# One order of weight loads two tiles ahead, the last block's sums over three groups, output weights reloaded in pairs, 28 tiles joined early

## The chip, the cores and the metric

The kernel runs on one core of one Trainium2 chip. The metric is the device time of one execution in microseconds (us), as the median of several executions. Engines: PE is TensorE (matmuls), PEld its weight loads, DVE is VectorE, ACT is ScalarE, POOL is GpSimd, and SP is the queue that issues nearly all DMAs. Each engine runs its instructions in the order of the program.

## What is computed

The reference has three parts, one after the other. Inputs q, k and v are float32, all weights are float64.

```python
# retention, 4 batches, 8 heads, 576 positions, 64 per head
scores = (1 / sqrt(64)) * q @ k.T
ret = scores * Dmat            # gamma[h] ** (i - j) for i >= j, else 0
x = (ret @ v)                  # 2304 tokens x 512
# first expert block: w1, w2, w3 are 512 x 768, w_out is 768 x 512
h = max(max(x @ w1, x @ w2), x @ w3)
x = h @ w_out
# second expert block: w_gate, w_val are 512 x 1536, w_out is 1536 x 512
g = x @ w_gate
out = (g * sigmoid(g) * (x @ w_val)) @ w_out
```

## The kernel before, in words

**Precision.** Every large product is made of three float32r matmuls: an operand is split into a high part (ACT copy to float32r) and a low part (DVE or POOL subtract), and high times low, low times high and high times high are added in PSUM. A float64 weight tile (128 partitions x 512, 512 KB) is first joined to float32 from its two words: `f32_steps` (L110) has two ACT operations (L114, L117) and three of DVE (L119, L120, L122). `conv_steps` (L125) adds the split.

**Order.** The program order of all engines is written by hand (`tc.manual_schedule`). Generators carry side work, and `next(...)` at fixed places advances them by one step.

**Stage 1, attention, 32 visits** (`visit`, L371). One visit does the attention of one unit (pair of heads, half a sequence) and, from visit 8, some slices of the first expert block (`f_slice`, L337: 12 matmuls, then ACT L351 or DVE L353 reads the PSUM tile, of which there are two). From visit 16 on each visit has five slices and also advances `early` (L406) two steps before the first slice and one before each later one and at the end, seven in all. `early` joins 22 tiles of the second expert block (tile rows 1 to 11 of w_gate and w_val) and stores the float32 result to `l_d` in DRAM (L417); a tile takes four steps, and its result lies in `wl`, of which there are two (L116). Loads run two tiles ahead; the float64 tile `w64` has three buffers (L103). At even visits `t_load` (L173) puts eight small DMAs on SP.

**Stage 2, remaining slices** (L507): what is left of the slices, while `wo_steps` (L473) loads, joins and splits the six tiles of the first w_out. Its first load is asked for here.

**Stage 3, first output product** (L659 to L691): six half blocks `hx` of 384 tokens, each with four sums `e` of 18 matmuls (L673). After each sum ACT reads it (L678), then `h_split` (L497: ACT high part, POOL low part) makes the operands of the next half block ((0, 1), (2,), (3, 4), (5,) for e = 0 to 3), then four steps of `xsteps` (sums and splits of the block's operands for the next stage) and two of `w_steps([0])`, the preparation of weight tile row 0 of the second expert block: loads (`w_load`, L546), three joins, four sums (L587 to L594) and five splits (L567), each stored to `w_d`.

**Stage 4, second expert block** (`group`, L729). One group takes a tile row `fi` and a block `b` of 768 tokens: seven products of six matmuls (L743) into three PSUM tiles g1 to g3, in the Strassen-like form with operands a, b, c, d, and the gate on ACT, DVE and POOL; then up to three `o()` calls, each an output sum `out2` of six matmuls (L703) of an older pair of tile rows, taken from the list `pend`. Between them ten `hook()` calls advance side work. The order is `seq` (L804): blocks 0 and 1 for all twelve tile rows, and then block 2 alone for tile rows 10, 11, 8, 9, 6, 7, 4, 5, 2, 3, 0, 1, whose weights come back from `w_d` by `w_reload` (L539): a, c, d, b into one buffer for even and one for odd rows, and p (output weights) into four (`wp0` to `wp3`).

In the first group `hook` runs two steps of `x_second(2)`, the last block's sums and splits, whose results go through `xt` (two buffers) and DMA to `x_d` (L626); two of its five splits have their low part on POOL, three on DVE. In the second group `w_steps([1])` runs, again two steps a hook. After that each tile row prepares the next one.

In the last block each group is followed by

```python
        if fi >= GRP:
            w_reload(fi - GRP, "acdbp")
```

Of the kernel before, what the change touches and what calls it, by code (L numbers as in the profile page):

```python
# [22 lines left out]
P = 128  # L23
# [10 lines left out]
GRP = 2  # L34
# [33 lines left out]
def retention_moe(ctx, tc, consts, q, k, v, w1, w2, w3, w_out, w_gate, w_val, w_out2, out):  # L68
# [302 lines left out]
    def visit(n, slices, convs):  # L371
        low = a_value(n)
        if n % 2:
            a_load(n // 2 + 3)
        else:
            t_load(n // 2 + 2)
        if n % (2 * NP) == 2 * NP - 1:
            fq.extend((n // NP - 1 + h, *w) for w in win_units for h in range(2))
        a_state(n + 1)
        low()  # L380
        a_score(n + 1)
        plan = list(conv_plan(convs))
        done = 0
        for j in range(slices + 1):
            if j == min(2, slices - 1) or not slices:
                a_prep(n + 2)
            upto = len(plan) * (j + 1) // (slices + 1)
            for step in plan[done:upto]:
                for i, ph in step:
                    win_phase(i, ph)  # L390
            done = upto
            if n >= 16:
                for _ in range(2 if j == 0 else 1):
                    next(early, None)
            if j < slices:
                f_some(1)

    EARLY = [(fi, wi) for fi in range(1, F2) for wi in range(2)]
# [6 lines left out]

    def early_steps():  # L406

        ld = {}
        last = None
        for i, x in enumerate(EARLY):  # L410
            for y in range(i, min(i + 3, len(EARLY))):
                if y not in ld:
                    ld[y] = load_w(late_src(*EARLY[y]))
            box = []
            for j, _ in enumerate(f32_steps(ld[i], box)):
                if j == 1 and last:
                    sp.dma_start(out=l_d[last[0]], in_=last[1])  # L417
                yield
            last = (x, box[0])
            yield  # L420
        sp.dma_start(out=l_d[last[0]], in_=last[1])
        yield
# [27 lines left out]
    for n in range(NU):  # L450
# [10 lines left out]
        if n < 8:  # L461
            spin(1)
    for _ in early:
        pass
# [8 lines left out]
    def wo_steps():  # L473

        ld = {}
        for i in range(F1):
            for j in range(i, min(i + 2, F1)):
                if j not in ld:
                    ld[j] = load_w(w_out[j * P:j * P + P, :])
            hi = hw.tile([P, 512], F32R, name="woh", tag="wo", bufs=2 * F1)  # L480
            lo = hw.tile([P, 512], F32R, name="wol", tag="wo", bufs=2 * F1)
            for _ in conv_steps(ld.pop(i), hi, lo, dve):
                yield
            wo.append((hi, lo))
            yield
# [47 lines left out]
    def wr_tile(fi, nm):  # L533
        w = dict(WOPS)[nm]
        tag = f"wp{fi % 4}" if nm == "p" else f"w{nm}"
        t = wop[(fi, nm)] = wr[fi % 2].tile([P, 2, w], F32R, name=f"w{nm}", tag=tag)
# [6 lines left out]
    ld2 = {}  # L543
    seq2 = [(fi, wi) for fi in range(F2) for wi in range(3)]

    def w_load(i):  # L546
        if i < len(seq2) and i not in ld2:
            x = seq2[i]
            if x in l_d:
                t = stg.tile([P, 512], U64, name="w64", tag="w64")  # L550
                ld2[i] = t.bitcast(F32)[:, 0:512]
                sp.dma_start(out=ld2[i], in_=l_d[x])
            else:
                ld2[i] = load_w(late_src(*x))

    def l_steps(i, box):

        for j in range(i, i + 3):
            w_load(j)
        t = ld2.pop(i)  # L560
        if seq2[i] in l_d:
            box.append(t)
        else:
            yield from f32_steps(t, box)
            yield
# [11 lines left out]
    def w_steps(fis):  # L577

        for fi in fis:
            box = []  # L580
            yield from l_steps(3 * fi, box)
            yield from l_steps(3 * fi + 1, box)
# [18 lines left out]
            yield from l_steps(3 * fi + 2, box)  # L601
# [13 lines left out]
    def x_split(b, nm, src, eng=dve):  # L615
# [3 lines left out]
        else:  # L619
            h, l = [xf.tile([P, 2, HT], F32R, name="xt", tag="xt", bufs=2) for _ in range(2)]  # L620
        act.activation(h, src, ACTF.Copy)
        yield
        eng.tensor_tensor(l, src, f(h), ALU.subtract)
        if b == NBK - 1:
            for y, t in enumerate((h, l)):
                sp.dma_start(out=x_d[(nm, y)], in_=f(t))  # L626
# [7 lines left out]
    def x_second(b, r):  # L634
# [14 lines left out]
        yield from x_split(b, "T2", t1)  # L649
        yield from x_split(b, "B22", r["B22"])  # L650
        yield from x_split(b, "T4", t3)
# [7 lines left out]
    for hx in range(NHX):  # L659
# [5 lines left out]
        for e in range(KD):  # L665
            ps = ps_mm.tile([P, 512], F32, name="ps2", tag="mm")
            n = 0
            for fi in range(F1):
# [3 lines left out]
                for l, rr in ((wh, hl), (wl, hh), (wh, hh)):  # L672
                    pe.matmul(ps[:, 0:HT], l[:, es], rr, start=n == 0, stop=n == 3 * F1 - 1)  # L673
                    n += 1
            nm = RAW[(e // 2, half)]
# [3 lines left out]
            for fi in ((0, 1), (2,), (3, 4), (5,))[e]:  # L679
                if hx + 1 < NHX:  # L680
                    h_split(*hq.pop(0))
                    if len(hq) > 3:
                        h_load(*hq[3])
            for _ in range(4):
                next(xsteps, None)
            if hx or e:
# [119 lines left out]
    steps = xsteps  # L806
    for fi, b in seq:
        if fi == 0 and b == 1:
            for _ in steps:
                pass  # L810
            steps = w_steps([1])
        if (fi, b) == (1, 0):
            xf_cm.__exit__(None, None, None)
            accp.append(ctx.enter_context(tc.tile_pool(name="acc", bufs=1, reuse_waits="tile")))
        if b == 0 and 0 < fi < F2 - 1:
# [6 lines left out]
        pace = 2 if fi == 0 or fi == F2 - 2 and b == 0 else 1  # L822

        def hook():
            for _ in range(pace):
# [9 lines left out]
    for fi in seq:  # L835
        group(fi, NBK - 1, lambda: None, fi == seq[-1])
        if fi >= GRP:
            w_reload(fi - GRP, "acdbp")
# [26 lines left out]
```

## Time and profile before

| what | value |
|---|---|
| median of 3 executions | 895.33 us (894.78 to 896.79) |
| profiled execution, its own time | 899.1 us |
| its span, first to last instruction | 897.3 us |
| mean granted TensorE clock | 0.971 of full speed |
| PE busy | 839.4 us, 94% |
| DVE, ACT, POOL busy | 561.9, 315.1, 222.8 us |
| DMA queue of SP | 137.10 MB |

Busy times are sums over the whole span. The clock column of a stretch gives the share of full speed that TensorE was granted there. An idle time of an engine is put down to whatever ended it last.

### The profile page before, as it was taken

To read this page: it belongs to the slowest core of one execution; us is meant where nothing else is said; L and a number is where in the kernel's file an instruction comes from. 1 tells how busy PE (TensorE), PEld (TensorE's weight loads), DVE (VectorE), ACT (ScalarE), POOL (GpSimd) and SP (SyncE) were. 2 spreads that over 40 slices of the span, in tenths; PEclk is the share of its full clock that TensorE was granted. 3 is DMA by queue.
4 is the path that set the end of the run, shared out by engine and by line. 5 is a ranking of instruction groups with operands and counts; after the bars stand their busy time and mean duration, and the time that the engine had idled before them with its cause. 6 is when DMAs were issued, how large, how long until landed. Compare 5 with 4: busy or idle time off the path is not lost.

```text
span 897.3 us, 15434 instructions
## 1 busy us (share of the span) xinstructions
PE 839.4 (94%) x5925; PEld 782.4 (87%) x5933; DVE 561.9 (63%) x988; ACT 315.1 (35%) x629; POOL 222.8 (25%) x209
## 2 busy tenths in 40 slices
PE   8899989999999899899859999999999999889888
PEld 6788878999999899899759999999998999788776
DVE  2659935777663352575388779999997554453435
ACT  2544413322221232564344553344433223321120
POOL 4233410000000012444233233333332222222121
PEclk9999998999999999999989999999999999998989
DMA  9999556879830334552464444444414246324531
GB/s 183 225 210 197 129 116 191 202 204 204 226 111 28 121 110 113 178 162 68 192 219 153 153 153 153 153 153 153 150 51 166 101 167 247 152 111 161 210 130 70
DMA packets 161913, 138.48 MB, mean 154 GB/s; under 512 B 101040, under 2 KB 135344, under 8 KB 161840
## 3 DMA queue, kind: packets, MB, share of 16 engines
q1 hardware_dynamic: 160480, 137.10, 52.0%
q8 instruction: 46, 0.75, 0.4%
q10 hardware_dynamic: 1360, 0.41, 0.2%
q14 instruction: 27, 0.22, 0.1%
HBM read 90.81 MB, written 46.66 MB: 153 GB/s over the span
## 4 chain that ended last, share of the span: by engine, by line
PE 57%; issue 15%; DVE 9%; DMA 7%; POOL 7%; SPq 3%; ACT 2%; POOLq 0%; DVEq 0%; ACTq 0%
PE ps L347 21%; PE g L743 16%; PE ps L720 10%; PE ps L673 4%; POOL gl L789 3%; POOL p L762 2%; PE s L244 2%; PE o_ps L285 2%; SPq L184 2%; PE o_ps L281 1%; POOL hl L502 1%; DVE wz L120 1%; DVE wl L122 1%; DMA x_dT<-xt 1%; DMA wc<-w_d5c 1%
## 5 line engine op out<-in xcount | busy, mean ns | idle before, releaser
L347 PE MATMUL ps<-xl,wh 128*128 128x288 f32 x576 | 175.3, 304 | 14.5 <-ACT hmax L351 9.3
L347 PE MATMUL ps<-xh,wh 128*128 128x288 f32 x576 | 171.4, 298 | 0.0
L347 PE MATMUL ps<-xh,wlo 128*128 128x288 f32 x576 | 171.4, 297 | 0.0
L789 POOL TENSOR_TENSOR gl<-p,gh 128x384 fp32r<-128x384 f32 x72 | 84.9, 1195 | 291.1 <-ACT gh L788 291.1
L720 PE MATMUL ps<-wp,gh 128*128 128x512 f32 (+1 forms) x436 | 135.7, 393 | 0.4 <-DVE acc L725 0.3
L347 PEld LDWEIGHTS ps<-xl,wh 128*128 128x128 f32 x576 | 109.7, 190 | 19.1 <-ACT hmax L351 10.0
L347 PEld LDWEIGHTS ps<-xh,wlo 128*128 128x128 f32 x576 | 109.9, 191 | 0.0
L347 PEld LDWEIGHTS ps<-xh,wh 128*128 128x128 f32 x576 | 109.8, 191 | 0.0
L720 PEld LDWEIGHTS ps<-wp,gh 128*128 128x128 f32 x436 | 80.7, 188 | 14.4 <-DVE acc L725 1.0
L353 DVE TENSOR_TENSOR hmax<-ps,hmax 128x288 f32<-128x288 f32 x96 | 43.6, 455 | 69.8 <-PE ps L347 58.7
L720 PE MATMUL ps<-wp,gl 128*128 128x512 f32 (+1 forms) x218 | 85.6, 393 | 0.0
L725 DVE TENSOR_TENSOR acc<-ps,acc 128x512 f32<-128x512 f32 (+1 forms) x91 | 62.1, 684 | 33.7 <-PE ps L720 32.3
L743 PE MATMUL g<-xhB,wa 128*128 128x384 f32 x288 | 77.4, 351 | 0.0
L743 PE MATMUL g<-xhT,wc 128*128 128x384 f32 x288 | 76.5, 348 | 0.0
L743 PE MATMUL g<-xlB,wa 128*128 128x384 f32 x144 | 52.1, 362 | 24.7 <-ACT p L753 12.4
L502 POOL TENSOR_TENSOR hl<-hf,hh 128x384 fp32r<-128x384 f32 x36 | 40.3, 1135 | 131.2 <-ACT hh L501 115.0
L788 ACT ACTIVATE gh<-p 128x384 fp32r<-128x384 f32 x72 | 37.8, 525 | 79.1 <-DVE p L792 53.9
L214 POOL TENSOR_TENSOR ks<-kn,cst_a 96x384 f32<-96x384 f32 (+1 forms) x32 | 24.6, 774 | 134.8 <-PE m_ps L260 116.9
L777 ACT ACTIVATE sb<-u 128x384 f32<-128x384 f32 x36 | 18.9, 525 | 105.6 <-DVE u L775 105.6
L743 PEld LDWEIGHTS g<-xhB,wa 128*128 128x128 f32 x288 | 55.6, 200 | 0.0
L743 PEld LDWEIGHTS g<-xhT,wc 128*128 128x128 f32 x288 | 55.1, 198 | 0.0
L673 PE MATMUL ps<-hl,woh 128*128 128x384 f32 x144 | 49.8, 346 | 4.8 <-ACT B L678 2.4
(119 smaller groups left out, 1671.7 us busy)
## 6 DMA issues: line engine op xcount, KB each, us to landing
w<-in_moe_w_out_dram SPq DMA_DIRECT2D x18, 512.0 KB, 4.1
h_d<-hmax SPq DMA_DIRECT2D x48, 144.0 KB, 2.4
w<-in_moe_w_dram SPq DMA_DIRECT2D x12, 512.0 KB, 6.2
w<-in_moe_w_gate_dram SPq DMA_DIRECT2D x12, 512.0 KB, 5.0
w<-in_moe_w_val_dram SPq DMA_DIRECT2D x12, 512.0 KB, 5.0
l_d<-wl SPq DMA_DIRECT2D x22, 256.0 KB, 4.9
w<-l_d SPq DMA_DIRECT2D x22, 256.0 KB, 3.0
vn<-in_v_dram SPq DMA_DIRECT2D x16, 288.0 KB, 5.9
```

The costliest lines, as they stand in the source:

```text
L184: sp.dma_start(out=t["t"][g:g + 32, i], in_=src[b, 2 * pr + e, :, 32 * x:32 * x + 32].rearrange("(a p) d -> p a d", p=32))
L214: pool.tensor_tensor(u["ks"][:, 0:nk], u["k"][:, 0:nk], sc, ALU.mult)
L347: pe.matmul(ps, l[:, ksl], r, start=n == 0, stop=n == 3 * KD - 1)
L353: dve.tensor_tensor(mx[hb], ps, mx[hb], ALU.max)
L502: pool.tensor_tensor(hl, hf, f(hh), ALU.subtract)
L673: pe.matmul(ps[:, 0:HT], l[:, es], rr, start=n == 0, stop=n == 3 * F1 - 1)
L720: pe.matmul(ps[:, cs], l[:, sl], r[:, cs], start=n == 0, stop=n == 3 * GRP - 1)
L725: dve.tensor_tensor(a[:, cs], ps[:, cs], a[:, cs], ALU.add)
L743: pe.matmul(ps, l[:, ks], r[:, kc], start=first and n == 0, stop=n == 5, skip_group_check=True)
L777: act.activation(sb, u2, ACTF.Sigmoid)
L788: act.activation(gh[half], t, ACTF.Copy)
L789: pool.tensor_tensor(gl[half], t, f(gh[half]), ALU.subtract)
```

## The change

Five edits: (1) one list of all weight loads, `ask` and `take`, always two tiles ahead, across the stages; the first two early loads are asked for at the end of visit 15; (2) `early` joins 28 tiles instead of 22 (also tile row 0, and output weights of rows 0, 1, 2 and 11), nine steps a visit instead of seven; (3) in stage 3 the splits stand ahead of the ACT read, and 3, 4, 5 go together, with three `xt` buffers, earlier stores, and `w_steps` only in some half blocks; (4) the last block's sums and splits go one step every other hook over the first three groups, all five low parts on POOL, while `w_steps([1])` runs one step a hook from the first group on and `w_steps([2])` waits until the fourth; (5) in the last block the output weights are reloaded two rows at a time after odd rows, and rows 8 and 9 not at all.

```diff
             if n >= 16:
-                for _ in range(2 if j == 0 else 1):
+                for _ in range(1 if j % 2 else 2):
                     next(early, None)
...
-    EARLY = [(fi, wi) for fi in range(1, F2) for wi in range(2)]
+    EARLY = [(fi, wi) for fi in range(F2) for wi in range(3) if wi < 2 or fi < 3 or fi == F2 - 1]
...
+    def ask(k):
+
+        while asked[0] <= min(k, NQ - 1):
+            i = asked[0]
+            asked[0] += 1
+            if i < NE:
+                queue[i] = load_w(late_src(*EARLY[i]))
+            elif i < NO:
+                j = i - NE
+                queue[i] = load_w(w_out[j * P:j * P + P, :])
+            else:
+                x = divmod(i - NO, 3)
+                if x in l_d:
+                    t = stg.tile([P, 512], U64, name="w64", tag="w64")
+                    queue[i] = t.bitcast(F32)[:, 0:512]
+                    sp.dma_start(out=queue[i], in_=l_d[x])
+                else:
+                    queue[i] = load_w(late_src(*x))
+
+    def take(k, ahead):
+        ask(k + ahead)
+        return queue.pop(k)
...
     def early_steps():
...
+            t = take(i, 2)
...
+        if n == 15:
+            ask(1)
...
     def wo_steps():
...
+            t = take(NE + i, 2)
...
-        t = wop[(fi, nm)] = wr[fi % 2].tile([P, 2, w], F32R, name=f"w{nm}", tag=tag)
+        t = wop[(fi, nm)] = wr[1 if fi % 2 or (nm == 'p' and fi % 4) else 0].tile([P, 2, w], F32R, name=f"w{nm}", tag=tag)
...
+    def l_steps(fi, wi, box):
+
+        t = take(NO + 3 * fi + wi, 1 if wi == 1 else 2)
+        if (fi, wi) in l_d:
             box.append(t)
...
-            h, l = [xf.tile([P, 2, HT], F32R, name="xt", tag="xt", bufs=2) for _ in range(2)]
+            h, l = [xf.tile([P, 2, HT], F32R, name="xt", tag="xt", bufs=3) for _ in range(2)]
         act.activation(h, src, ACTF.Copy)
+        if b == NBK - 1:
+            sp.dma_start(out=x_d[(nm, 0)], in_=f(h))
         yield
         eng.tensor_tensor(l, src, f(h), ALU.subtract)
         if b == NBK - 1:
-            for y, t in enumerate((h, l)):
-                sp.dma_start(out=x_d[(nm, y)], in_=f(t))
+            sp.dma_start(out=x_d[(nm, 1)], in_=f(l))
...
-        yield from x_split(b, "T2", t1)
-        yield from x_split(b, "B22", r["B22"])
-        yield from x_split(b, "T4", t3)
+        yield from x_split(b, "T2", t1, side)
+        yield from x_split(b, "B22", r["B22"], side)
+        yield from x_split(b, "T4", t3, side)
...
+            for fi in ((0, 1), (2,), (), (3, 4, 5))[e]:
+                if hx + 1 < NHX:
+                    h_split(*hq.pop(0))
+                    if len(hq) > 3:
+                        h_load(*hq[3])
             nm = RAW[(e // 2, half)]
             if nm not in r:
                 r[nm] = raw(nm)
             act.activation(r[nm][:, e % 2], ps[:, 0:HT], ACTF.Copy)
-            for fi in ((0, 1), (2,), (3, 4), (5,))[e]:
-                if hx + 1 < NHX:
-                    h_split(*hq.pop(0))
-                    if len(hq) > 3:
-                        h_load(*hq[3])
-            for _ in range(4):
+            for _ in range(4 if e < 2 else 3):
                 next(xsteps, None)
-            if hx or e:
+            if half or hx == 0:
                 next(steps, None)
                 next(steps, None)
...
-    steps = xsteps
-    for fi, b in seq:
-        if fi == 0 and b == 1:
-            for _ in steps:
+    beat = [0]
+    for j, (fi, b) in enumerate(seq):
+        if j == 3:
+            for _ in xsteps:
                 pass
-            steps = w_steps([1])
-        if (fi, b) == (1, 0):
             xf_cm.__exit__(None, None, None)
...
-        if b == 0 and 0 < fi < F2 - 1:
+        if b == 0 and fi < F2 - 1:
             for _ in steps:
                 pass
             steps = w_steps([fi + 1])
...
-        pace = 2 if fi == 0 or fi == F2 - 2 and b == 0 else 1
+        pace = 0 if j == 2 else 2 if j == 3 or fi == F2 - 2 and b == 0 else 1
 
         def hook():
+            beat[0] += 1
+            if j < 3 and beat[0] % 2:
+                next(xsteps, None)
             for _ in range(pace):
                 next(steps, None)
...
         if fi >= GRP:
-            w_reload(fi - GRP, "acdbp")
+            w_reload(fi - GRP, "acdb")
+        if fi % GRP and GRP < fi < F2 - 1:
+            for ci in range(GRP):
+                w_reload(fi - 2 * GRP + 1 + ci, "p")
```

## Rows read from the trace of the kernel before

**Rows 1.** The page, part 1: busy time, share of the span, instructions.
```profile
PE 839.4 (94%) x5925; PEld 782.4 (87%) x5933; DVE 561.9 (63%) x988; ACT 315.1 (35%) x629; POOL 222.8 (25%) x209
```

**Rows 2.** The waits of PE: releaser, us in total, times, longest us.
```profile
PE g L743 <- ACT p L753: 12.4, 4, 7.0
PE ps L347 <- ACT hmax L351: 9.3, 3, 5.6
...
PE g L743 <- DVE p L769: 3.8, 1, 3.8
PE g L743 <- DMA wa<-w_d7a: 3.3, 1, 3.3
...
PE ps L673 <- ACT B L678: 2.4, 1, 2.4
PE ps L673 <- POOL hl L502: 2.4, 3, 1.8
```

**Rows 3.** Stages: length, busy of PE, PEld, DVE, ACT, POOL; clock, DMA share, GB/s.
```profile
131.00:146.00 15.00, 9.64 (x84) 9.25 (x84) 5.57 (x12) 3.82 (x9) 0.40 (x1) 0.77 0.57 176
146.00:264.00 118.00, 117.91 (x1172) 112.41 (x1169) 82.83 (x182) 36.64 (x76) 7.37 (x11) 1.00 0.80 200
348.00:431.80 83.80, 79.02 (x433) 77.65 (x432) 44.56 (x44) 41.34 (x80) 34.25 (x30) 0.96 0.48 146
431.80:486.40 54.60, 39.78 (x189) 37.66 (x189) 38.76 (x60) 23.95 (x46) 15.93 (x12) 0.87 0.52 191
742.03:765.04 23.01, 23.01 (x121) 21.40 (x121) 11.28 (x21) 7.67 (x15) 6.56 (x6) 1.00 0.63 229
765.04:879.08 114.04, 101.09 (x476) 91.99 (x476) 48.33 (x83) 25.39 (x51) 25.61 (x24) 0.91 0.39 150
```

**Rows 4.** The chain that ended last, from visit 16: start us, us, what.
```profile
130.65 4.11 DMA w<-in_moe_w_gate_dram
...
136.35 7.45 PE ps L347 x36
...
146.12 8.16 PE ps L347 x60
```

**Rows 5.** The timeline of SP at the start of visit 16.
```profile
126.27 2.12 SPq L184 DMA_DIRECT2D qk<-in_k_dram  x4
```

**Rows 6.** The timeline of PE; in brackets the idle time before and its releaser.
```profile
301.71 0.40 PE L347 MATMUL ps<-xl,wh 128*128 128x288 f32 x1 [3.15 <-ACT hmax L351]
...
687.56 0.44 PE L743 MATMUL g<-xlB,wa 128*128 128x384 f32 x1 [1.39 <-ACT p L753]
```

**Rows 7.** The chain that ended last, in stage 3.
```profile
394.11 11.73 PE ps L673 x57
...
421.82 10.16 PE ps L673 x57
```

**Rows 8.** Groups by line: count, busy us, mean ns, idle before them.
```profile
L120 DVE SCALAR_TENSOR_TENSOR wz<-w,wz 128x512 uint32<-128x512 uint32 x54 | 40.4, 748 | 1.8
...
L623 DVE TENSOR_TENSOR xt<-B,xt 128x768 fp32r<-128x768 f32 x4 | 3.8, 958 | 8.7 <-DMA x_dB<-xt 4.9 <-DMA x_dT<-xt 2.4 <-ACT xt L621 1.4
...
L623 POOL TENSOR_TENSOR xt<-t,xt 128x768 fp32r<-128x768 f32 x1 | 1.8, 1838 | 12.6 <-ACT xt L621 12.6
```

**Rows 9.** The timeline of SP in the last block.
```profile
775.14 0.32 SPq L541 DMA_DIRECT2D wp<-w_d6p  x1
775.51 0.42 SPq L541 DMA_DIRECT2D wa<-w_d7a  x1
```

**Rows 10.** The waits of SP's queue: us in total, times, longest us.
```profile
SPq L541 <- PE ps L720: 84.0, 4, 22.0
```

**Rows 11.** DMA issues: count, KB each, median us to landing.
```profile
l_d<-wl SPq DMA_DIRECT2D x22, 256.0 KB, 4.9
...
wa<-w_d4a SPq DMA_DIRECT2D x1, 512.0 KB, 8.7
```

**Rows 12.** The waits of ACT: us in total, times, longest us.
```profile
ACT wl L117 <- DMA l_d<-wl: 22.0, 10, 5.5
```

More of the change, by code (lines that the diff above doesn't have):

```diff
@@ L404, in late_src @@
         return cols((w_gate, w_val)[wi], fi * P)
+    NE = len(EARLY)
+    NO = NE + F1
+    NQ = NO + 3 * F2
+    queue = {}
+    asked = [0]
+    def ask(k):
[18 more added lines that the diff above has]
+        return queue.pop(k)
     def early_steps():
-        ld = {}
         last = None
         for i, x in enumerate(EARLY):
-            for y in range(i, min(i + 3, len(EARLY))):
-                if y not in ld:
-                    ld[y] = load_w(late_src(*EARLY[y]))
+            t = take(i, 2)
             box = []
-            for j, _ in enumerate(f32_steps(ld[i], box)):
+            for j, _ in enumerate(f32_steps(t, box)):
                 if j == 1 and last:
@@ L473, in wo_steps @@
     def wo_steps():
-        ld = {}
         for i in range(F1):
-            for j in range(i, min(i + 2, F1)):
-                if j not in ld:
-                    ld[j] = load_w(w_out[j * P:j * P + P, :])
+            t = take(NE + i, 2)
             hi = hw.tile([P, 512], F32R, name="woh", tag="wo", bufs=2 * F1)
             lo = hw.tile([P, 512], F32R, name="wol", tag="wo", bufs=2 * F1)
-            for _ in conv_steps(ld.pop(i), hi, lo, dve):
+            for _ in conv_steps(t, hi, lo, dve):
                 yield
@@ L541, in w_reload @@
             sp.dma_start(out=f(wr_tile(fi, nm)), in_=w_d[(fi, nm)])
[L543 to L561, printed above, removed]
+    def l_steps(fi, wi, box):
+        t = take(NO + 3 * fi + wi, 1 if wi == 1 else 2)
+        if (fi, wi) in l_d:
             box.append(t)
@@ L580, in w_steps @@
             box = []
-            yield from l_steps(3 * fi, box)
-            yield from l_steps(3 * fi + 1, box)
+            yield from l_steps(fi, 0, box)
+            yield from l_steps(fi, 1, box)
             lg, lv = box
@@ L600, in w_steps @@
             box = []
-            yield from l_steps(3 * fi + 2, box)
+            yield from l_steps(fi, 2, box)
             yield from split(fi, "p", box[0])
```

## The prediction, made before the change was run

> **What bounds the kernel now.** I read the page first. PE is busy 94% of the span [rows 1], so what can be won is PE's idle time, some 58 us, and the time that it spends at its lower clock. The waits of PE say where it idles [rows 2]; the stage table says what each place costs with the clock [rows 3]. In visits 16 to 28 (146 to 264 us) and in a pair of last-block groups (742 to 765) PE is busy throughout at full clock: nothing is to be had there. The losses lie in five places, all at the seams of stages: the first early load, the first w_out load, the first output product, the first three groups of stage 4, and the weight reloads of the last block. A sixth is one small wait in stage 4.
>
> A stall costs more than its idle time. In stage 3 the 57 recorded matmuls after a stall of 1.8 us took 11.73 us, 57 undisturbed ones 10.16 [rows 7]: 1.6 us more at the lower of the two clocks (1.2 instead of 2.4 GHz). I use 1.6 us per stall where no row of the place itself is at hand.
>
> **The change part by part.**
>
> *First early load.* SP issues eight `t_load` DMAs from 126.27 on [rows 5] and then, at 130.65, the first float64 load, which lands 4.1 us later [rows 4]; ACT waits for it, a read of a full PSUM tile stands behind it, and PE idles 5.6 us [rows 2]. The 36 matmuls after it take 7.45 us; at the rate of the 60 that took 8.16 [rows 4] they would take 4.9. Together 8.1 us. Now two loads are issued ahead of the eight DMAs, 4.4 us earlier (130.65 - 126.27). Load, ACT's two operations and PE's restart all move by that, so some 1.2 us of idle time stay, and perhaps half of the slow 2.6 us. I take **-5.5** (bounds -4.0, -8.1).
>
> *First w_out load.* PE idles 3.15 us at 301.7 [rows 6] because the load is asked for only when its join is due. In the one list it is asked for while the last early tiles are joined, two visits before. **-3.2**; late next is nothing, the loads after it are two ahead as well.
>
> *First output product.* Four idle times, 2.4 and 2.4 us together [rows 2], and two of them are followed by a slow stretch of 1.6: 8.0. The first is ACT waiting for float64 loads of tile row 0; those joins move to stage 1, and the joined tiles are loaded before the stage begins. The others are a low part from POOL that comes late, since ACT's split of tile 5 stood behind the PSUM read of the last sum; now it stands ahead of it. Tile 3 can be split once PE has used the buffer, half a microsecond into the fourth sum. Fewer preparation steps lie in the busy half blocks. **-7** (bounds -5, -8).
>
> *First groups of stage 4.* The stretch from 431.8 takes 54.6 us for four groups and three output sums. A pair of groups with six output sums is 84 matmuls of 384 columns and 36 of 512, 50,688 columns, in 23.0 us [rows 3]: 7.3 us a group, 1.4 an output sum. The floor is 4 x 7.3 + 3 x 1.4 = 33.5. DVE is the rival: its 60 operations took 38.8 us, 0.65 each [rows 3]. Two joins (six operations) and three low parts go away, so 51 are left, 33 us: as much as PE's floor, but unevenly. The first group holds its own 8, three sums and the first seven operations of `w_steps([1])`: 18 x 0.65 = 11.7 against PE's 7.3. The second has 8 + 1 + 2 = 11 (7.1), the third 8 (5.2), the fourth 17 (11.0 against 11.5). So DVE falls 4.4 us behind once, ACT's first read of the next group stands behind the late gate, and PE, which covers a part with three products, idles in the second and third groups; DVE catches up in the third. I count the lag once, 4.4, and two slow stretches of 1.6: 41.1, so **-13.5**; I take **-13** (bounds -4, -19). POOL gets three low parts more. It needs 1.84 us for one, DVE 0.96 [rows 8].
> The Trainium skill, GPSIMD Engine Reference, section Engine selection, says to keep two-input elementwise work on VectorE because GpSimd is about twice as slow; the rows agree (1.9 times). By that rule alone the move would cost 3 x 0.88 = 2.6 us instead of the nothing that I count.
>
> *The small wait.* At 687.56 PE idles 1.39 us [rows 6] behind a group in which DVE also joins the output weights of row 11. That tile is now joined in stage 1. **-1.4**.
>
> *Reloads of the last block.* SP issues p of row 6 at 775.14 and a of row 7 right behind it [rows 9]: p waits until PE has made the last output sum with the old contents, and a, needed when group 7 starts, stands behind it. SP waited 84.0 us in four such places [rows 10], and PE idles 3.3 us for a of row 7 [rows 2], similarly for rows 5, 3 and 1. Eight groups take 114.0 us where four undisturbed pairs take 92.0 [rows 3]: 22.0 lost. Now a, c, d and b of row 7 go to SP ahead of any p, a whole group before they are needed. What waits behind p of rows 6 and 7 is a of row 4, issued at the same 775 to 776 us. It is needed when group 7 ends, some 12 us later; with ten reloads in the queue it took 8.7 us to land [rows 11], and now five are ahead of it or beside it. p of rows 8 and 9 is still in its buffer. **-22** (bounds -17, -23).
>
> *Six more joined tiles in stage 1.* Each is 512 KB in, 256 KB out, two ACT and three DVE operations of at most 0.75 us [rows 8]. All 28 end in the same visit as the 22 did, at nine steps a visit (some 10.2 us) instead of seven. PE itself loses nothing to the joins while ACT and DVE keep up (36.6 and 82.8 of 118 us busy); DMA share goes from 0.80 by a fifth, 4.7 on 23.6 MB, to 0.96 [rows 3]. The tight place is `wl`: ACT already waits ten times, 22.0 us, for the store of an old `wl` to land [rows 12], which takes 4.9 us [rows 11], behind the eight DMAs of each even visit on SP. The six steps between a join and the reuse of its buffer shrink from 8.8 to 6.8 us, so these waits grow by 2 us. Two PSUM tiles cover ACT for a slice, 1.6 us, more. Six of the bursts fall into these visits; I take 1 us each, **+6** (bounds 0, where the cover holds, and 6 x (2.0 + 1.6) = 22).
>
> **The sum.** -5.5 - 3.2 - 7 - 13 - 1.4 - 22 + 6 = -46.1. The profiled execution took 899.1 us, so 853.0; it was 3.8 longer than the median of 895.33, so a median of about **849**.
>
> **The rivals.**
> *A: stage 1 pays.* DMA at 0.96 of its time and ACT's waits reach PE in each burst: +22 instead of +6, 865. For it: ACT's waits of up to 5.5 us [rows 12]; against: not one of them reached PE (117.91 of 118 us busy).
> *B: POOL in the way.* Five low parts of 1.84 us in three groups stand ahead of POOL's add, which PE's last product waits for through DVE (3.8 us once already, [rows 2]): 9.2 us more, 858. Against: POOL's own six operations of a pair take 6.6 us [rows 3], 3.3 a group, so with 3.1 more it stays under 7.3.
> The Trainium skill's page GPSIMD Engine Reference, section Specifications, bears on it: GpSimd shares its SBUF interfaces with VectorE, and operations with two SBUF inputs contend.
> *C: the queue stays blocked.* If a of row 4 lands over 3.5 us later than the 8.7 allow, the stall only moves to the even groups, three times (5.5 us each as now): 849 + 16.5 = 866.
> *D: slower than before.* In stage 1 all 28 tiles wait as long as the longest now, 5.5 us, and PE idles for what exceeds the 1.6 of cover: 28 x 3.9 = 109, which less the 52.1 won gives 952. It decides from a mean of 52.1 / 28 = 1.9 us of stall a tile, 3.5 us of wait. Against: that mean is 2.2 now over ten tiles, nought over twelve.
> *E: the edits do less than they say,* the early loads still blocked by the stores ahead of them on SP and stage 3 waiting for POOL as before: 849 + 12 = 861.
>
> **How the numbers follow.** Forecast 0.60 (own range 838 to 857), A 0.16, B 0.08, C 0.07, E 0.05, D 0.04. The low end takes the forecast with stage 1 free and the first groups near their floor (33.5 for 41.1): 849 - 6 - 7 = 836. The high end takes in A and C with a little on top, 870. A measurement of this kernel tells some 0.2%, 1.8 us. All cases but D are faster by far more; of D a small part would end near no change: faster 0.95, same 0.01, slower 0.04.
>
> **What would show it.** Right: no wait of PE for a reload, eight groups at 765 to 879 taking about 92 us; the stretch of four groups about 41; no idle time at the w_out load; ACT's waits on `l_d` well above 22 us. Wrong: PE idle inside visits 16 to 28 by over 10 us, PE waiting for POOL in the first groups, or waits for a of rows 4, 2 and 0.

## The result, and the profile after

The kernel after takes 855.64 us (median of four executions, 851.17 to 858.38), the kernel before, run beside it, 896.06: a ratio of 0.9543 [0.9497, 0.9588]. The forecast was 849.0 with a range of 836 to 870. The profiled execution took 856.3 us where the one of before took 899.1: 42.8 less, forecast 46.1.

PE is now busy for nearly the whole span (94% in [rows 1]). The page's part 1 after:

```profile
PE 825.5 (97%) x5933; PEld 768.3 (90%) x5933; DVE 553.3 (65%) x985; ACT 313.7 (37%) x629; POOL 231.6 (27%) x212
```

To see where the 42.8 us came from, cut both spans at the same places of the program, by PE's timeline (the first attention matmul of a visit, the first product of stage 3 and of stage 4, the last product of a group), and compare piece by piece. "Visits 17 to 28" runs from the start of visit 17 to the start of visit 28, "visits 29 to 31" from there to the start of visit 31, "rest to stage 3" from there on:

| piece | before | after | change | forecast |
|---|---|---|---|---|
| visit 16 (first early load) | 18.6 | 11.9 | -6.7 | -5.5 |
| visits 17 to 28 (joins) | 114.3 | 125.3 | +11.0 | +6 |
| visits 29 to 31 | 26.2 | 26.2 | 0 | 0 |
| rest to stage 3 (first w_out load) | 62.9 | 58.0 | -5.0 | -3.2 |
| stage 3 | 83.9 | 78.4 | -5.5 | -7 |
| first four groups of stage 4 | 54.4 | 43.6 | -10.9 | -13 |
| the 24 groups after them (small wait) | 278.8 | 276.6 | -2.2 | -1.4 |
| eight groups of the last block (reloads) | 114.0 | 90.8 | -23.2 | -22 |
| sum | | | -42.5 | -46.1 |

The same pieces in the view by windows (columns as in [rows 3]), after: visit 16, visits 17 to 28, stage 3, the first four groups, the last eight.

```profile
125.60:137.50 11.90, 10.58 (x108) 9.91 (x106) 6.84 (x16) 3.34 (x7) 0.82 (x1) 1.00 0.90 212
137.50:262.80 125.30, 117.45 (x1146) 110.51 (x1144) 88.28 (x190) 41.98 (x85) 8.28 (x11) 0.99 0.88 231
347.00:425.40 78.40, 76.28 (x435) 74.68 (x434) 34.09 (x36) 38.18 (x74) 35.79 (x30) 1.00 0.47 143
425.40:468.90 43.50, 37.29 (x187) 35.05 (x187) 32.41 (x49) 20.78 (x41) 22.20 (x15) 0.92 0.56 209
745.50:836.40 90.90, 90.90 (x477) 84.41 (x476) 48.38 (x83) 25.01 (x51) 25.78 (x24) 1.00 0.48 172
```

The last line is the plainest: PE is busy for 90.90 of 90.90 us at full clock, where [rows 3] has 101.09 of 114.04 at 0.91. The second line is the one place that got worse: PE is 7.85 us idle in visits 17 to 28, and busy 3.2 us longer than before, part of it at the lower clock (last section). The kernel before in the same visits:

```profile
144.40:258.70 114.30, 114.21 (x1146) 108.78 (x1144) 79.13 (x173) 35.31 (x73) 7.78 (x11) 1.00 0.82 204
```

The fourth line of after still has a clock of 0.92 and 6.2 us of idle time.

The waits of PE after (releaser, us in total, times, longest us), beside [rows 2]:

```profile
PE ps L347 <- DVE hmax L353: 11.1, 11, 2.6
PE g L754 <- ACT p L764: 5.8, 3, 2.2
PE ps L347 <- ACT hmax L351: 2.4, 3, 1.3
PE ps L684 <- POOL hl L527: 2.1, 3, 0.9
```

The wait for the reload (DMA wa) is gone and the ACT wait of the first load has fallen from 5.6 to 1.3. What has grown is the first line: PE waits for DVE to read the slices' PSUM tile, in stage 1. The kernel before has that wait too, all of it ahead of visit 16:

```profile
PE ps L347 <- DVE hmax L353: 5.1, 4, 2.6
```

In after 7.3 of the 11.1 us lie in visits 17 to 28. ACT's and DVE's waits and those of SP's queue say why, and what became of the blocked queue ([rows 12, 10]):

```profile
ACT wl L117 <- DMA l_d<-wl: 57.5, 23, 7.2
DVE wl L122 <- ACT wl L117: 8.7, 5, 2.8
```

```profile
SPq L566 <- PE ps L731: 38.8, 8, 9.5
SPq L566 <- PE g L754: 35.3, 15, 4.0
```

ACT waits 57.5 us, not 22.0, for the stores out of `wl` before it may write the buffer again. DVE's last operation of a join then waits for ACT (8.7 us, 0.5 before), and the read of a slice's PSUM tile, for which PE waits, stands behind that operation in DVE's order. SP still waits for PE before it can issue reloads, 74.1 us in 23 places, but no place is long (9.5 against 22.0), and PE waits for no reload behind one.

### The profile page after: what moved, and what is told of

It is laid out like the page before. It is cut to its first block, busy times and chain, and to the rows that moved or that the text cites. A ratio compares the mean times of both kernels' runs of the same rounds, so it can differ in the third digit from the quotient of the medians.

```text
span 854.5 us, 15491 instructions
## 1 busy us (share of the span) xinstructions
PE 825.5 (97%) x5933; PEld 768.3 (90%) x5933; DVE 553.3 (65%) x985; ACT 313.7 (37%) x629; POOL 231.6 (27%) x212
## 4 chain that ended last, share of the span: by engine, by line
PE 47%; issue 18%; DMA 10%; DVE 10%; POOL 8%; SPq 4%; ACT 3%; POOLq 0%; DVEq 0%; ACTq 0%
PE g L754 17%; PE ps L347 13%; PE ps L731 11%; DMA l_d<-wl 5%; POOL gl L800 4%; SPq L184 2%; PE ps L684 2%; POOL hl L527 2%; POOL p L773 2%; DVE wl L122 1%; DVE wz L120 1%; DMA qk<-in_q_dram 1%; DVE hmax L353 1%; PE o_ps L285 1%; PE s L244 1%
## 5 line engine op out<-in xcount | busy, mean ns | idle before, releaser
L347 PE MATMUL ps<-xl,wh 128*128 128x288 f32 x576 | 175.2, 304 | 13.5 <-DVE hmax L353 11.1
L754 PE MATMUL g<-xhB,wa 128*128 128x384 f32 x288 | 73.8, 337 | 0.0
L754 PE MATMUL g<-xhT,wc 128*128 128x384 f32 x288 | 73.2, 335 | 0.0
L117 ACT ACTIVATE wl<-w 128x512 uint32<-128x512 uint32 x54 | 36.1, 669 | 62.4 <-DMA l_d<-wl 57.5
L754 PE MATMUL g<-xlB,wa 128*128 128x384 f32 x144 | 49.1, 341 | 5.8 <-ACT p L764 5.8
L754 PEld LDWEIGHTS g<-xhB,wa 128*128 128x128 f32 x288 | 52.2, 188 | 0.0
L754 PEld LDWEIGHTS g<-xhT,wc 128*128 128x128 f32 x288 | 52.0, 188 | 0.0
```

Of the source, the lines that this page charges most:

```text
L117: act.activation(l, u[:, :, 0], ACTF.Copy, scale=float(2.0 ** -29))
L347: pe.matmul(ps, l[:, ksl], r, start=n == 0, stop=n == 3 * KD - 1)
L754: pe.matmul(ps, l[:, ks], r[:, kc], start=first and n == 0, stop=n == 5, skip_group_check=True)
```

## Experiments

Twelve kernels, each timed beside the kernel before. All but the last three change one place of the program (wl3 also the warm-up matmuls), and the table gives every piece as above (us), from one profiled execution each. Pieces that an edit does not touch show how much they vary from kernel to kernel: visits 17 to 28 at the nine steps of after take 121.7 to 126.6, and the four groups in the six kernels that share after's code there 42.1 to 43.9.

| kernel | median | ratio [95%] | v16 | v17-28 | rest | stage 3 | 4 groups | middle | last 8 |
|---|---|---|---|---|---|---|---|---|---|
| before | 896.06 | 1 | 18.6 | 114.3 | 62.9 | 83.9 | 54.4 | 278.8 | 114.0 |
| after | 855.64 | 0.9543 [0.9497, 0.9588] | 11.9 | 125.3 | 58.0 | 78.4 | 43.6 | 276.6 | 90.8 |
| no_ask15 | 861.27 | 0.9586 [0.954, 0.9631] | 18.6 | 125.4 | 58.0 | 78.4 | 43.9 | 276.7 | 90.8 |
| reload_alone | 874.31 | 0.9742 [0.97, 0.9784] | 17.9 | 114.3 | 62.6 | 82.5 | 55.3 | 278.9 | 90.9 |
| wl3 | 850.22 | 0.9471 [0.9428, 0.9514] | 11.9 | 117.1 | 58.0 | 78.4 | 43.0 | 276.7 | 90.8 |
| pace7 | 846.77 | 0.9439 [0.9396, 0.9481] | 11.8 | 114.3 | 60.3 | 78.4 | 42.1 | 276.7 | 90.8 |
| p_late | 858.98 | 0.9569 [0.9536, 0.9602] | 11.7 | 124.9 | 58.0 | 78.4 | 45.3 | 278.4 | 90.8 |
| split_order_undone | 852.36 | 0.9492 [0.9466, 0.9517] | 11.7 | 123.0 | 58.0 | 76.4 | 42.2 | 276.6 | 90.8 |
| spread_undone | 862.17 | 0.9594 [0.955, 0.9638] | 12.0 | 126.6 | 58.0 | 78.5 | 47.7 | 276.8 | 90.6 |
| old_chain | 864.82 | 0.9632 [0.9604, 0.9661] | 12.0 | 121.7 | 58.0 | 78.4 | 52.3 | 276.9 | 90.6 |
| low_dve | 854.46 | 0.9512 [0.9477, 0.9546] | 11.7 | 123.2 | 58.0 | 78.4 | 42.6 | 276.7 | 90.8 |
| mixed_even | 849.46 | 0.946 [0.9433, 0.9486] | 12.0 | 114.3 | 58.0 | 78.4 | 47.6 | 276.6 | 90.8 |
| best_low_dve | 842.97 | 0.939 [0.9364, 0.9416] | 11.9 | 114.3 | 58.0 | 76.4 | 43.9 | 276.7 | 90.8 |
| best | 843.02 | 0.9387 [0.9359, 0.9415] | 11.7 | 114.3 | 58.0 | 76.4 | 42.1 | 276.7 | 90.8 |

Visits 29 to 31 take 26.2 us in each.

### The first early load: no_ask15

```diff
-        if n == 15:
-            ask(1)
```

> The changed kernel without the two loads asked for at the end of visit 15. Theory (the load stood behind eight small DMAs on SP): visit 16 takes 17.5 to 18.6 us instead of 11.9, with a stall of some 5.6, median 861 to 863. Rival (the single order of loads would have done it): visit 16 stays at 12 to 13, median 855 to 857.

Visit 16 takes 18.6 us again, all else is as after: asking two loads ahead of the eight small DMAs is worth 6.7 us by itself. PE's timeline of this kernel and then of after, at the first slice that waited:

```profile
135.84 0.61 PE L347 MATMUL ps<-xl,wh 128*128 128x288 f32 x1 [5.37 <-ACT hmax L351]
```

```profile
131.90 0.40 PE L347 MATMUL ps<-xl,wh 128*128 128x288 f32 x1 [1.32 <-ACT hmax L351]
```

### The reloads: reload_alone

The kernel before with edit 5 alone.

```diff
-            w_reload(fi - GRP, "acdbp")
+            w_reload(fi - GRP, "acdb")
+        if fi % GRP and GRP < fi < F2 - 1:
+            for ci in range(GRP):
+                w_reload(fi - 2 * GRP + 1 + ci, "p")
```

> The kernel before with the reload edit alone. Theory (p ahead of a in SP's queue was the whole loss): the eight groups of the last block that took 114.0 us take 91 to 92, no wait of PE for a reload, median 896 - 22 = 874. Rival (the queue stays blocked, the stall moves to the even groups): three waits of some 3 us for a of rows 4, 2, 0 with slow stretches, median about 890.

The eight groups take 90.9 us and PE has no idle time over 0.35 us in them; the other pieces stay near before. So the whole 23.2 is edit 5's, and no stall moved to the even groups: rival C is out. The stretch from 747 to 863 us, eight groups and what follows, by windows (columns as in [rows 3]):

```profile
747.00:863.00 116.00, 115.72 (x595) 105.96 (x594) 61.61 (x105) 31.63 (x63) 31.34 (x29) 1.00 0.49 172
```

### The joins in stage 1: wl3 and pace7

Two theories for the 11 us of visits 17 to 28: the reuse of `wl` (ACT waits for the store of the tile before last), or the sheer volume of DMA. wl3 gives every third early tile a buffer of its own; to make room the operand of the warm-up matmuls is 320 columns wide instead of 512, with more of them.

```diff
-        l = stg.tile([P, 512], U32, name="wl", tag="wl", bufs=2)
+        if third:
+            l = att.tile([P, 512], U32, name="wle", tag="wle", bufs=1)
+        else:
+            l = stg.tile([P, 512], U32, name="wl", tag="wl", bufs=2)
...
-            for j, _ in enumerate(f32_steps(t, box)):
+            for j, _ in enumerate(f32_steps(t, box, i % 3 == 2)):
```

> The changed kernel with a third wl buffer for every third early tile (and a shorter warm-up tile, to make room). Theory (ACT waits for the store of an old wl, and its lateness reaches PE): ACT's waits on l_d fall from 57.5 us to under 15, visits 17 to 28 take 114 to 117 us instead of 125.3, median about 847. Rival (the DMA engines themselves are at their limit, share 0.88): the wait moves to the tile loads, visits 17 to 28 stay at 122 or more, median 853 to 858.

pace7 goes back to the seven steps a visit of before; the joins then end some visits later.

```diff
-                for _ in range(1 if j % 2 else 2):
+                for _ in range(2 if j == 0 else 1):
```

> The changed kernel with seven early steps a visit instead of nine, so that the 28 tiles spread over visits 16 to 31. Theory (the rate of joins, six steps of a visit between the end of a join and the reuse of its buffer, is too high): visits 17 to 28 take 114 to 117 us, visits 29 to 31 stay at some 8.7 us each, median about 847. Rival (any 28 tiles cost this much because of what they load): the loss is spread over the visits, 17 to 31 together lose the same 11 us, median 853 to 858.

With the third buffer the visits take 117.1 us: 8.2 of the 11 are gone. ACT's waits within these visits, in after (137.5 to 262.8 us) and then in wl3 (138.3 to 255.5):

```profile
ACT wl L117 <- DMA l_d<-wl: 56.1, 22, 7.2
...
ACT wz L114 <- DMA w<-in_moe_w_out_dram: 4.3, 1, 4.3
```

```profile
ACT wl L120 <- DMA l_d<-wl: 5.5, 4, 2.2
ACT wz L114 <- DMA w<-in_moe_w_out_dram: 5.5, 2, 4.8
...
ACT wz L114 <- DMA w<-in_moe_w_gate_dram: 1.5, 2, 1.1
ACT wz L114 <- DMA w<-in_moe_w_val_dram: 1.3, 3, 0.6
```

The store wait has nearly gone (56.1 to 5.5), and ACT waits longer for the loads of the float64 tiles (8.3 us against 4.3). The visits in wl3 and then in best, which has pace7's seven steps there, by windows:

```profile
138.30:255.50 117.20, 114.85 (x1150) 108.90 (x1146) 88.20 (x191) 42.95 (x85) 7.79 (x11) 1.00 0.93 247
```

```profile
139.30:253.60 114.30, 114.21 (x1146) 108.78 (x1144) 79.68 (x174) 36.58 (x75) 7.78 (x11) 1.00 0.86 215
```

At nine steps a visit DMA is busy for 0.93 of the time and 3 us stay, with ACT waiting for loads; at seven steps and 0.86 PE loses nothing, as before the change, though all 28 tiles are joined. So the reuse of the buffer cost 8 us, and the other 3 go with the rate of nine steps, not with the volume as such. That it is the loads that cost these 3 is argued from the waits; no run shows it by itself. In pace7 ACT still waits for the stores, but in the cover of the PSUM tiles:

```profile
ACT wl L117 <- DMA l_d<-wl: 29.0, 13, 5.2
```

It wins 8.9 us of the median. What it gives back is one stall where the joins run on into the stretch after the visits, 2.3 us longer (60.3):

```profile
285.13 0.40 PE L347 MATMUL ps<-xl,wh 128*128 128x288 f32 x1 [2.05 <-ACT hmax L351]
```

### Which tiles are joined early: p_late

26 tiles: the output weights of rows 1 and 2 are joined in stage 4 again.

```diff
-    EARLY = [... if wi < 2 or fi < 3 or fi == F2 - 1]
+    EARLY = [... if wi < 2 or fi in (0, F2 - 1)]
```

> The changed kernel with 26 joined tiles: the output weights of rows 1 and 2 are joined in the first groups again. Theory (two joins of 1.9 us on DVE where DVE lags): four groups 45 to 47 us instead of 43.5, while visits 17 to 28 take 2 to 4 us less than 125, median 855 to 857. Rival (DVE has room there): four groups at 43 to 44, median 851 to 853.

The first four groups take 1.7 us more and the middle 1.8 (1.41 of it one idle time of PE in the fifth group). Visits 17 to 28 take no less (124.9 against 125.3), with ACT's waits for stores hardly fewer:

```profile
ACT wl L117 <- DMA l_d<-wl: 51.6, 22, 5.4
```

The 2 to 4 us less that were expected there did not come, but these visits vary by 5 us among kernels with the same joins, so two tiles fewer decide nothing. pace7 does: 28 tiles at seven steps cost nothing. The price in stage 1 goes by the rate, nine steps a visit, and not by the number of tiles.

### The order of the splits in stage 3: split_order_undone

```diff
-            for fi in ((0, 1), (2,), (), (3, 4, 5))[e]:
...
             act.activation(r[nm][:, e % 2], ps[:, 0:HT], ACTF.Copy)
+            for fi in ((0, 1), (2,), (3, 4), (5,))[e]:
...
```

> The changed kernel with the splits of stage 3 behind the PSUM read again, tiles 3 and 4 at the third sum, 5 at the fourth. Theory (the order shortened POOL's late low parts): stage 3 takes 80.5 to 82 us instead of 78.4, with waits of PE for hl of over 3 us in all, median 858 to 860. Rival (the joined tiles and the lighter half blocks did all of it): 78 to 79, median 855 to 856.

Stage 3 takes 76.4 us, 2.0 less than after, and 76.4 again in both kernels below that share this edit: the order that the change brought costs time. Neither theory had foreseen less than 78. POOL's timeline at such a place, in after and then in split_order_undone (start us, us; in brackets the idle time before):

```profile
384.80 6.10 POOL L527 TENSOR_TENSOR hl<-hf,hh 128x384 fp32r<-128x384 f32 x5 [5.72 <-ACT hh L526]
```

```profile
381.39 2.01 POOL L527 TENSOR_TENSOR hl<-hf,hh 128x384 fp32r<-128x384 f32 x2 [2.88 <-ACT hh L526]
384.06 1.01 POOL L527 TENSOR_TENSOR hl<-hf,hh 128x384 fp32r<-128x384 f32 x1 [0.67 <-ACT hh L526]
387.84 1.99 POOL L527 TENSOR_TENSOR hl<-hf,hh 128x384 fp32r<-128x384 f32 x2 [2.76 <-ACT hh L526]
```

In after POOL is idle for 5.72 us and then has five low parts in a row, to 390.90; the next half block's first sum needs them earlier, and PE waits:

```profile
389.01 0.44 PE L684 MATMUL ps<-hl,woh 128*128 128x384 f32 x1 [0.88 <-POOL hl L527]
```

Left in pairs, the same low parts are spread over the sums. The edit takes back two things, the place ahead of the read and the lot of three; the rows point to the lot, but no run parts them.

### The first groups: spread_undone, old_chain, low_dve

spread_undone takes back the order of edit 4: the last block's sums and splits run in the first group, `w_steps([1])` in the second, two steps a hook. The three `xt` buffers, the earlier stores, POOL's low parts and the early tiles stay.

```diff
-        if b == 0 and fi < F2 - 1:
+        if j == 1:
+            for _ in xsteps:
+                pass
+            steps = w_steps([1])
+        if b == 0 and 0 < fi < F2 - 1:
...
-        pace = 0 if j == 2 else 2 if j == 3 or fi == F2 - 2 and b == 0 else 1
+        pace = 2 if fi == 0 or fi == F2 - 2 and b == 0 else 1
...
-            beat[0] += 1
-            if j < 3 and beat[0] % 2:
-                next(xsteps, None)
             for _ in range(pace):
-                next(steps, None)
+                next(xsteps if j == 0 else steps, None)
```

> The changed kernel with the last block's sums and splits in the first group again and the preparation of tile row 1 in the second, two steps a hook (three xt buffers, low parts on POOL and the joined tiles kept). Theory (the spreading took most of the 10.9 us that the four groups got shorter): four groups take 50 to 54 us instead of 43.5, median 862 to 866. Rival (the third buffer, earlier stores and the missing joins did it): four groups at 43 to 46, median 855 to 858.

old_chain takes back, besides, the third `xt` buffer, the earlier store and three of the five low parts on POOL.

```diff
-... name="xt", tag="xt", bufs=3 ...
+... name="xt", tag="xt", bufs=2 ...
-        yield from x_split(b, "T2", t1, side)
+        yield from x_split(b, "T2", t1)
...
```

> The spreading undone, and besides two xt buffers, both stores after the low part and three low parts on DVE, as before the change; only the joined tiles and the order of loads stay of the change in the first groups. Theory (each split waited for the stores of the one before, 2.3 us each, and this chain in DVE's and ACT's order was what the buffers shortened): four groups 51 to 54 us against 47.7 with the spreading alone undone, median 866 to 869. Rival (the joined tiles did it): 47 to 49, median 862 to 864.

The four groups go 54.4 (before), 52.3 (old_chain), 47.7 (spread_undone), 43.6 (after). Read as steps: the joins and loads moved out of them give 2.1 us, the third buffer with the stores and POOL's low parts 4.6, the new order 4.2, each with some 1 us of scatter. The 47.7 lies between theory and rival of spread_undone: order and buffers both have a share. PE's longer idle times there, in old_chain:

```profile
433.17 0.69 PE L753 MATMUL g<-xlT,wb 128*128 128x384 f32 x1 [4.04 <-DVE p L779]
446.12 0.69 PE L753 MATMUL g<-xlB,wa 128*128 128x384 f32 x1 [6.92 <-ACT p L763]
457.58 0.44 PE L753 MATMUL g<-xlB,wa 128*128 128x384 f32 x1 [2.01 <-ACT p L763]
```

and in after:

```profile
438.23 0.44 PE L754 MATMUL g<-xlB,wa 128*128 128x384 f32 x1 [2.25 <-ACT p L764]
449.02 0.44 PE L754 MATMUL g<-xlB,wa 128*128 128x384 f32 x1 [1.64 <-ACT p L764]
458.47 0.44 PE L754 MATMUL g<-xlB,wa 128*128 128x384 f32 x1 [1.87 <-ACT p L764]
```

Three waits, 13.0 us in all, have become three of 5.8. low_dve puts three of the low parts back on DVE, to ask whether POOL is what remains:

```diff
-        yield from x_split(b, "T2", t1, side)
-        yield from x_split(b, "B22", r["B22"], side)
-        yield from x_split(b, "T4", t3, side)
+        yield from x_split(b, "T2", t1)
+        yield from x_split(b, "B22", r["B22"])
+        yield from x_split(b, "T4", t3)
```

> The changed kernel with the low parts of T2, B22 and T4 back on DVE (as before the change). Theory from the prediction (DVE is what lags in the first groups, POOL has room): three operations of 0.96 us more on DVE, four groups 45 to 47 us instead of 43.5, median 857 to 859. Rival (POOL's low parts hold DVE up: L802 took 2.04 us beside one instead of 0.54, and L658 waited for one): four groups 40 to 42, median 852 to 854.

The stretch takes 42.6 us against 43.6, but with no edit there it takes 42.1 in pace7 and 43.9 in no_ask15: inconclusive, and neither theory's number. Repeated on a faster kernel it is 43.9 (best_low_dve) against 42.1 (best), with medians 0.05 us apart. Where these low parts run makes no difference that could be measured.

### The best of both: mixed_even and best

mixed_even has pace7's seven steps up to visit 26 and nine after it, so that the joins end inside stage 1, and starts the preparation of weight row 1 five hooks later, to thin DVE's work in the first group.

```diff
-                for _ in range(1 if j % 2 else 2):
+                for _ in range(2 if j == 0 or n >= 27 and j % 2 == 0 else 1):
...
-            for _ in range(pace):
+            for _ in range(0 if beat[0] <= 5 else pace):
```

> A version meant to beat both: seven early steps a visit up to visit 26 and nine after, and the preparation of tile row 1 begins five hooks later, so that DVE's work is more even over the first two groups. Theory: visits 17 to 28 at 114 to 115 us as with seven steps, the stretch from visit 31 to stage 3 at 58 as with nine, four groups at 40 to 42 us, median 842 to 845. Rival (the preparation then lands in the second group and DVE lags there): four groups at 43 to 45, median 846 to 848.

The pace does what it should: 114.3 and 58.0, the stall of pace7 is gone. The later start is a miss: the four groups take 47.6, with idle times of 3.30 and 3.64 us; by the place of these stalls the work is only pushed into groups that DVE enters late already.

best is after with that pace and with the order of the splits of before (the edit of split_order_undone); best_low_dve adds low_dve's.

> A version meant to beat both: the changed kernel with seven early steps a visit up to visit 26 and nine after, and with the splits of stage 3 behind the PSUM read as before. Theory (the two parts that cost time in the change are independent of the rest): visits 17 to 28 at 114.3 us, from visit 31 to stage 3 at 58.0, stage 3 at 76.4, four groups at 42 to 44, median 842 to 845. Rival (the stages trade with each other): median 847 or more.

> The version before with the low parts of T2, B22 and T4 on DVE too. If POOL's low parts hold DVE up, four groups are 1 to 2 us shorter than in that version, median 1 to 2 below it; if DVE is what lags, 2 to 3 longer; if neither, within 1 us.

best takes 843.02 us (840.47 to 843.71), 0.9387 [0.9359, 0.9415] of before, and is faster than both kernels; its execution times do not overlap with those of after. By pieces it wins 11.0 in visits 17 to 28 and 2.0 in stage 3 over after.

## Why the prediction was right, and where its steps were not

The prediction's order of sizes held: two pieces, the reloads and the first groups, gave 34 of the 42.5 us, and stage 1 paid. Its profile sum was 3.3 us too optimistic. That this is so little is in part luck: four pieces won 5.0 us more than forecast together, and three fell 8.6 short. The other half of the miss in the median is a correction: I took 3.8 us off for the distance of the profiled execution from the median, but the profiled execution of after lies only 0.7 above its own. That distance belongs to one execution and not to the kernel. Of the signs that the prediction named, the waits for reloads, the last eight groups, the w_out load and ACT's waits came as said; the four groups took 43.6, not about 41; and PE's idle time in visits 16 to 28, 9.2 us, stayed just under the 10 that would have spoken against it.

- **First early load** (-5.5, measured -6.7): right, no_ask15 gives it alone. The stall that stays is 1.32, as worked out (1.2), but no slow stretch follows it: the clock of visit 16 is 1.00, so nearly all of the slow 2.6 us came back, not half.
- **First w_out load** (-3.2, measured -5.0): mis-sized. I counted the idle time only and left out the slower matmuls after it, although I had charged them elsewhere. The window of the kernel before shows them: a clock of 0.97 over 63.0 us is 1.9 us.

```profile
284.90:347.90 63.00, 59.85 (x449) 59.48 (x446) 25.25 (x48) 18.08 (x37) 6.09 (x6) 0.97 0.30 96
```

- **First output product** (-7, measured -5.5): one of its reasons was wrong. "Now it stands ahead of it", the new order of the splits, costs 2.0 us; the other parts together, early joins and lighter half blocks among them, gave 83.9 - 76.4 = 7.5. I saw that tile 5's high part moved ahead, and not that giving 3, 4 and 5 out together sends POOL five low parts in one burst.
- **First groups** (-13, measured -10.9): the floor and the lag were right, the sentence "DVE catches up in the third" was not. The first stall is where I put it: PE is done with the group at 432.7, DVE's last gate operation ends at 437.25. But stalls follow in the third and fourth groups too. By after's rows: 33.5 of floor, 6.2 of idle time (2.25 + 1.64 + 1.87 + 0.46) and (1 - 0.92) x 43.5 = 3.5 for the clock make 43.2 of the 43.5 us. The 3.5 are the two slow stretches that were counted; the idle time is 6.2, not 4.4. Some of DVE's operations are held up by POOL (below), though low_dve shows no gain from moving POOL's low parts away. It was not foreseen that what comes with the order (buffer, stores, POOL) is worth as much as the order itself.
- **Small wait** (-1.4, measured -2.2 over 24 groups): the idle time of 1.39 us is gone, as said. Where the other 0.8 lies is not shown.
- **Reloads** (-22, measured -23.2): right in mechanism and size, and shown by itself.
- **Six more joined tiles** (+6, measured +11.0): the step that failed by most. I charged 1 us for each of six more bursts, although the working has the waits of all joins grow by 2 us. The price is set by the rate of all joins: ACT waited 23 times instead of 10. That is the mechanism of rival A at half its price; wl3 shows the part of the buffer, and pace7 that the rate is the measure and not the number of tiles.

Of the rivals, A had its place and cause right, but 11 us is half of its 22. B: PE's wait behind POOL's add and DVE, 3.8 us before ([rows 2]), does not occur in after; no wait of PE in the first groups names POOL. C is excluded by reload_alone. D is far off: ACT's 22 waits of 56.1 us in visits 17 to 28 left PE idle for 7.85 us there. E: no edit did less than it said, save for the split order, which went the wrong way.

Not settled: which of buffer, store and POOL's low parts in old_chain brings how much of the 4.6 us (they were changed together), what the 3 us are that wl3 leaves, and which half of the split order costs the 2.0. The low parts alone (low_dve) change nothing in the spread order, but that was not tried in the old one.

## What to carry to other kernels

On a queue that issues in order, sort requests by when they can start: one that must wait for a buffer belongs behind all that can go at once, and edit 5 alone is worth 23 us here. When side work is moved under a busy engine, what counts is its rate against the reuse of its buffers, so try the old pace with the new amount before paying for memory. Work handed out in larger lots can cost though nothing in it is new: look at the engine that receives the lot, not at the one that issues it.

## What was not expected of the hardware

Some DVE operations wait, in the middle of their own time, until POOL is through. The add at L802 (128x384, float32) takes 0.54 us when POOL is idle. In after it took 1.00 us where it began during a low part on POOL, and 2.04 us where it began just after one had started. In both cases it ended 0.4 us after POOL did. L780, which reads one of its inputs from PSUM (where PE's sums lie), took its usual 0.56 us in the middle of such a low part:

```profile
435.05 0.54 DVE L802 TENSOR_TENSOR u<-u,sb 128x384 f32<-128x384 f32 x1
440.99 2.28 POOL L635 TENSOR_TENSOR xt<-B,xt 128x768 fp32r<-128x768 f32 x1
441.85 0.56 DVE L780 TENSOR_TENSOR p<-g,p 128x384 f32<-128x384 f32 x1 [0.27 <-PE g L754]
443.35 2.62 POOL L635 TENSOR_TENSOR xt<-t,xt 128x768 fp32r<-128x768 f32 x1
445.38 1.00 DVE L802 TENSOR_TENSOR u<-u,sb 128x384 f32<-128x384 f32 x1 [0.65 <-ACT sb L788]
453.57 1.85 POOL L635 TENSOR_TENSOR xt<-B,xt 128x768 fp32r<-128x768 f32 x1
453.79 2.04 DVE L802 TENSOR_TENSOR u<-u,sb 128x384 f32<-128x384 f32 x1 [0.76 <-ACT sb L788]
```

In low_dve, where DVE does these low parts, the last of these adds takes 0.56 us:

```profile
454.10 0.56 DVE L802 TENSOR_TENSOR u<-u,sb 128x384 f32<-128x384 f32 x1 [0.65 <-ACT sb L788]
```

It is not only these. Counted over the whole trace of after, 69 `TENSOR_TENSOR` operations of DVE with no input in PSUM begin while POOL runs one; every one of them ends 0.28 us or more after POOL's, and the median takes 0.75 us longer than the fastest of its kind. The 79 with an input in PSUM take at most 0.02 us longer. So in these rows the two engines do not share the time: a DVE operation of this kind that comes second is held until POOL is through.

The Trainium skill, GPSIMD Engine Reference, section Specifications, says that the two engines share SBUF interfaces and that operations with two SBUF inputs contend; these rows agree, with a factor of up to 3.8, and low_dve and best_low_dve show no loss of the kernel's time from it.

The clock did not fall after every stall. The 5 us after five stalls of after, by windows (columns as in [rows 3]):

```profile
131.90:136.90 5.00, 5.00 (x38) 4.84 (x38) 3.88 (x9) 1.36 (x3) 0.00 (x0) 1.00 0.91 175
244.24:249.24 5.00, 5.00 (x26) 5.00 (x27) 3.60 (x8) 0.28 (x1) 0.00 (x0) 0.66 0.87 215
438.23:443.23 5.00, 5.00 (x20) 5.00 (x21) 3.81 (x6) 3.21 (x6) 4.63 (x3) 0.66 0.47 184
449.02:454.02 5.00, 5.00 (x29) 5.00 (x30) 2.32 (x5) 2.82 (x5) 4.16 (x4) 1.00 0.73 291
458.47:463.47 5.00, 4.54 (x16) 3.98 (x17) 4.46 (x9) 2.17 (x5) 2.17 (x2) 0.66 0.16 63
```

After the stalls of 1.32 us (visit 16) and 1.64 us (third group) the clock stays at 1.00, which is 2.4 GHz. After those of 2.59 us (the longest in visits 17 to 28), 2.25 and 1.87 us (first groups) it is 0.66, so PE spent part of these 5 us at 1.2 GHz, and (1 - 0.66) x 5 = 1.7 us of its speed are lost each time. The 1.6 us of the prediction has the right size for a slow stretch; what does not hold is that each stall brings one. Which stalls do, these rows do not settle.
